# Block-sparse attention and top-2 experts on one core: a weight split, a ring of raw weights and the first gathers are put elsewhere in the order

## The chip, the cores and the metric

The kernel runs on one core of a Trainium2 chip. The metric is device time in microseconds (us) of one execution; the time before is the median of three runs. One execution was also recorded by the hardware profiler, and all rows below are from that one.

## The reference

Block-sparse attention first: 4 batches of 8 heads, 768 rows, 64 columns a head, in blocks of 32 rows. A block of queries sees its neighbours, the first and last block and three sampled ones; the first and last block see everything.

```python
scores = scale * np.matmul(q, k.transpose(0, 1, 3, 2))
scores = np.where(mask, scores, -1000000000.0)
attn = softmax(scores)
attn_out = np.matmul(attn, v)
```

Its 3072 rows of 512 go to eight experts, two for each row, chosen by noisy gate logits:

```python
for e in range(8):
    for k in range(2):
        mask = top2[:, k] == e
        h = np.maximum(x[mask] @ w1[e], 0.0)      # 512 -> 1024
        out[mask] += top2_w[mask, k, None] * (h @ w2[e])   # 1024 -> 512
```

## The kernel before, in words

**Order.** The kernel writes out its own order: every engine runs its instructions in program order, and transfers go out on two queues, SP's (`nc.sync`) and POOL's (`nc.gpsimd`), each in its own order too. A transfer that has to wait holds all that stands behind it on its queue.

**Attention.** `Attention.steps` (line 482) walks 64 items, 16 a batch (12 "q" items, two for each tile of 128 queries, and 4 "g" items), as a pipeline: step k makes the scores and the softmax of item k+2, transposes the probabilities of item k and multiplies item k-1 with the values (`av`, line 350, L361; global blocks in `global_av`, L384). The values of a tile lie in `va` and `vb`; `prefetch_v` (line 212) loads a tile in two halves, the second a step after the first, by eight to fourteen transfers on SP's queue (L229, L234). The last batch is steps 46 to 63, and its tiles of values 2 to 5 go out at steps 54, 56, 58 and 60, their second halves a step later. `prefetch_k` copies keys of a tile from `kk` into `kc` on POOL (L206). `kk` has two buffers, `kk0` for batches 0 and 2, `kk1` for batches 1 and 3 (line 92). At the end of a step, after all of this, `step` (spot 3) does what `plan` holds for that step. `at(n, f, ...)` puts something there. In the code `NS` is 64, `PER` 16, `EC` 53 and `M0` 57. The router's work on a finished batch is spread over the steps as a generator; batch 2's ends in step 57 with the table of rows for units 0 and 1 (`finish_table`, `r_gi`, L835).

**Experts.** `Experts.units` is a list of ten units, each some rows of one expert. Units 0 and 1 are experts 0 and 1 over the rows of batches 0 to 2, units 2 and 3 the same experts' rows of batch 3, and unit 4 (`FAST`, expert 2) is the fifth. A unit gathers its rows from `x_rows` into `xg` (`gather`, POOL's queue, L1004), transposes them by DMA into `xta` or `xtb` (`xpose`, SP's queue, L1014), and runs a first layer and a second (`mm2`, L1157 and L1166). From unit 4 on the first layer is `layer1_fast` (line 1085): 28 products of six matmuls each in the order of `PRODUCTS` (numbered 0 to 27 here), seven products a column group with sums of blocks, and eight hooks at which other work is issued (`HOOKS`: hook 0 after product 3, hook 1 after product 6, hook 2 after product 10). ACT copies some products out of PSUM (L1098, `ta` and `tc`), and a later product that adds into the same bank waits for that copy.

**Weights.** A piece of raw weights is 128 x 1024 fp32 (512 KB). `load_piece` (line 909) loads it on SP's queue into one of three buffers of the pool `wst`. `weight_sums` (L921, four DVE additions) makes block sums of a first-layer piece from expert 2 on, `high_piece` (L946, ACT) and `low_piece` (L950, DVE) split the piece into two fp16 parts, after which the next load may take the buffer. `do` (line 1468) issues a list of such operations by short names, and first the loads whose buffers came free since the last call. `FIRST_BACK` says what is issued behind the two chunks of unit 3's second layer; behind a chunk `back` puts the transposes of unit 5's rows first, and then that list.

Of the kernel before, what the change touches and what calls it, by code (L numbers as in the profile page):

```python
# [9 lines left out]
F32 = mybir.dt.float32  # L10
# [10 lines left out]
P = 128  # L21
# [27 lines left out]
class Attention:  # L49
# [3 lines left out]
    def __init__(self, tc, qt, qg, kt, vx, vw, vg, sampled, H, D):  # L53
        self.tc, self.nc = tc, tc.nc
        self.qt, self.qg, self.kt, self.vx, self.vw, self.vg, self.sampled = qt, qg, kt, vx, vw, vg, sampled
        self.B, self.T = qt.shape[:2]
        self.H, self.D = H, D
        self.NP = H // 2
        self.S = self.T * P
        self.NB = self.S // 32  # L60
        self.W = D + 4
        self.HD = H * D
        self.HW = H * self.W
        self.late_ = (self.B - 1) * self.T
        self.RB = 32 * self.HD * 4
        self.held_v = {}
        self.listed_rows, self.weights = {}, {}
        self.items = []
        for b in range(self.B):
            q = [("q", b, t, f) for t in range(self.T) for f in range(2)]  # L70
            g = [("g", b, i, par) for i in range(2) for par in range(2)]
            self.items += g[0:2] + q[0:1] + g[2:3] + q[1:2] + g[3:] + q[2:] if b == 0 else q[0:1] + g[0:3] + q[1:2] + g[3:] + q[2:]
        self.st = {}

    def open(self, ctx, early, ident):
        tc, nc = self.tc, self.nc
        pool = lambda c, name, bufs, **kw: c.enter_context(tc.tile_pool(name=name, bufs=bufs, **kw))
        self.const = pool(ctx, "aconst", 1, side="right")
        self.buf = pool(ctx, "abuf", 1, side="right")
        self.qp = pool(ctx, "aq", 3, side="right")  # L80
        self.pp = pool(ctx, "app", 2, side="right")
        self.gp = pool(early, "agp", 3)
        self.sm = pool(ctx, "asm", 4, side="right")
        self.xp = pool(ctx, "axp", 2, side="right")
        self.ps_s = pool(ctx, "ps_s", 3, space=PSUM)
        self.ps_o = pool(ctx, "ps_o", 2, space=PSUM)
        ep = pool(early, "aeb", 1)
        two = lambda n: ep if n == 2 else self.buf
        J = self.NJ
        self.va = [two(i).tile([P, J, self.HW], F32, name=f"va{i}") for i in range(3)]  # L90
        self.vb = [two(i).tile([P, J, self.HW], F32, name=f"vb{i}") for i in range(3)]
        self.kk = [two(2 - 2 * i).tile([P, self.NB, P], F32, name=f"kk{i}") for i in range(2)]
        self.kc = [self.buf.tile([P, J, self.NP, 8, 32], F32, name=f"kc{i}") for i in range(2)]
        self.qgt = [two(2 - 2 * i).tile([P, self.NP, 64], F32, name=f"qg{i}") for i in range(2)]
        self.ends = [two(2).tile([P, self.HD], F32, name=f"ends{i}") for i in range(2)]
        self.xs = [self.buf.tile([P, self.NP, 2, P], F16, name=f"x{n}") for n in range(2)]
        self.og = self.const.tile([P, 4, self.W], F32, name="og")
        self.known = self.const.tile([P, self.NB, 2], F32, name="known")
        self.pgt = [self.buf.tile([P, 8, P], F32, name=f"pgt{i}") for i in range(4)]
        self.ident = ident  # L100
        self.ident16 = self.const.tile([P, P], F16, name="a_ident16")
        nc.vector.tensor_copy(self.ident16, self.ident)
        nc.vector.memset(self.known, 1.0 / XS)
        self.zero = self.const.tile([P, 256], F32, name="zero")
        nc.vector.memset(self.zero, 0.0)
# [736 lines left out]


class Experts:
    def __init__(self, tc, router, w1, w2, out, x_dram):
        self.tc, self.nc, self.router = tc, tc.nc, router
        self.w = (w1, w2)
        self.out, self.x_dram = out, x_dram
        self.N, self.D = out.shape
        self.KB = self.D // P  # L850
        self.FB = 2 * self.KB
        self.st = {}

        self.units = [(0, 0, CA), (1, 1, CA), (E + 1, 1, CB), (E, 0, CB)] + [(e, e, C) for e in range(NH, E)]
        self.w1b, self.w2b, self.tb = {}, {}, {}
# [10 lines left out]
    def open_left(self, ctx):  # L866
        tc = self.tc
        pool = lambda name, bufs, **kw: ctx.enter_context(tc.tile_pool(name=name, bufs=bufs, **kw))
        self.wst = pool("wst", 3)
        self.w1s = [pool("w1s", 1)]  # L870
        self.xp = pool("mxp", 1)
        self.xta = pool("mxta", 1)
        self.xg = self.xp.tile([P, 7, 2 * self.D], F16, name="xg")
        self.first = self.xg[:, 5:7, 0:CA]
# [32 lines left out]
        return u >= FAST  # L907

    def load_piece(self, e, i):
        t = self.wst.tile([P, 2 * self.D], F32, name="wraw")  # L910
        self.nc.sync.dma_start(t, self.w[i // 4][e, i % 4])
        self.st["wraw", e, i] = t

# [397 lines left out]
def kernel(ctx, tc, qt, qg, kt, vx0, vx1, vx2, vx3, vw, vg, sampled_blocks, gates, noise, w1, w2, out):  # L1311
    nc = tc.nc
    N, DM = out.shape
    T = qt.shape[1]
    H = 2 * qt.shape[3]
    x_dram = nc.dram_tensor("x_rows", (N, 2 * DM), F16, kind="Internal").ap()
# [2 lines left out]
    nc.scalar.preload_act_table_set("natural_log_exp_and_others")  # L1319
    rp = ctx.enter_context(tc.tile_pool(name="route", bufs=1))  # L1320
    router = Router(tc, rp, N, DM, T, x_dram)
    ex = Experts(tc, router, w1, w2, out, x_dram)
    att = Attention(tc, qt, qg, kt, (vx0, vx1, vx2, vx3), vw, vg, sampled_blocks, H, DM // H)
    late, early, left, right, first = (ExitStack() for _ in range(5))
    att.open(late, early, router.ident)
    router.hot = late.enter_context(tc.tile_pool(name="hot", bufs=1, side="right"))
    jobs = []

# [5 lines left out]
    def background(count=1):  # L1334
        for _ in range(count):
            if jobs and next(jobs[0], jobs) is jobs:
                jobs.pop(0)

    NS = len(att.items)
    PER = NS // att.B  # L1340
    EC = PER * 3 + 5
# [7 lines left out]
    at = lambda n, f, *a: plan.setdefault(n, []).append((f, a))  # L1349
# [4 lines left out]
    for i in range(8):  # L1354
        at(PER + 7 + 3 * i, fill_out, i)
    for i in range(3):
        at(EC + 1 + i, ex.load_piece, 0, i)
    at(NS - 4, ex.split_piece, 0, 0)
    at(NS - 3, ex.load_piece, 0, 3)
    M0 = NS - 7  # L1360
    at(M0, ex.meta, 0)
    at(M0 + 1, ex.meta, 1)
    for c in range(ex.count(0)):
        at(M0 + 2 + c // 2, gather_early, c)
        at(M0 + 3 + c // 2, ex.xpose, 0, c)

    for i in range(2):
        at(i - 2, router.consts, i)
# [5 lines left out]
    def step(n, spot):  # L1374
# [6 lines left out]
        for f, a in plan.get(n, []):  # L1381
# [22 lines left out]
    GATHERS = (((2, 0), (2, 1)), ((3, 0), (3, 1)), ((4, 4), (4, 5)), ((4, 6), (4, 0)), ((4, 1), (4, 2)))  # L1404
    FIRST_ROWS = ((), (), (), (("rs", 0, 0),), (("rs", 0, 1),), (("rd", 0, 0),), (("rd", 0, 1),),
                  (("rh", 0), ("rs", 1, 0), ("rs", 1, 1), ("rd", 1, 0), ("rd", 1, 1), ("rl", 0), ("rh", 1)))
    FIRST_BACK = ((("rl", 1), ("s2", 2), ("h2", 2), ("l2", 2)), (("s2", 3), ("h2", 3)))
    SPLITS = ((1, 2), (3,), (4,), (5,), (6,), (7,), (), ())
    queue = [(e, i) for e in range(E) for i in range(8)]

# [7 lines left out]
    def split(e, i):  # L1418
        ex.split_piece(e, i)
        next_load(e, i)  # L1420

    def low(e, i):
        ex.low_piece(e, i)
        freed.append((e, i))

    def front(u, f):
        nn = ex.count(u + 1) if u + 1 < nu else 0
        if u == 0:
            for i in SPLITS[f]:
                split(0, i)  # L1430
            background(UB if f else 0)
            if 1 <= f <= nn:
                ex.gather(1, f - 1)
            if 2 <= f <= nn + 1:
                ex.xpose(1, f - 2)
        if u == 1:
            if f < 3:
                background(UB if f < 2 else 200)
            else:
                ex.gather_prev(1, [f - 3])  # L1440
            if f == 4:
                nc.gpsimd.memset(ex.xg[:, C // P], 0.0)
                for v in (2, 3, 4):
                    ex.meta(v)
        if u == 2:
            if f == 1:
                ex.gather(4, 3)
            if FAST + 1 + f < nu:
                ex.meta(FAST + 1 + f)
        if u == 3:  # L1450
            if f in (2, 3):
                ex.gather_prev(3, [3 - f])
            for c in ((0, 1), (2, 3), (), (), (4,), (5,), (6,), ())[f]:
                ex.gather(5, c)
            do(u, FIRST_ROWS[f])
        if u == FAST:
            if f == 0:
                low(2, 3)
            if f > 3:
                ex.gather_prev(u, ex.chunks(u)[2 * f - 8:2 * f - 6])  # L1460
        if u == nu - 1 and f == 3:
            nc.gpsimd.drain()
        if u >= FAST:
            do(u, FRONT[f])
            if nn:
                do(u, FRONT_ROWS[f])
# [23 lines left out]
    def back(u, k, n):  # L1490
# [17 lines left out]
        if u == 3:  # L1508
            for c in range(4 * k, 4 + 3 * k):
                ex.xpose(5, c)  # L1510
            do(u, FIRST_BACK[k])
        if u >= FAST and nn:
# [4 lines left out]
    for u in range(nu):  # L1517
        left_ = ex.rows(u)[1]
        n = ex.count(u)
# [64 lines left out]
```

## Time and profile before

| | us |
|---|---|
| runs | 847.37, 847.04, 841.62 |
| median | 847.04 |
| the profiled execution | 847.43 |
| its span, first to last instruction | 845.6 |

Mean granted TensorE clock 0.978. Busy shares: PE 93%, DVE 69%, ACT 47%, POOL 46%. In the rows "[3.06 <-issue]" at the end of a line is the idle time of that engine ahead of it and what ended it; "issue" is time in which the engine waited for nothing that the profile shows. SPq is SP's DMA queue: the duration on its rows is that of the issue, not of the transfer.

### The profile page before, as it was taken

To read this page: it belongs to the slowest core of one execution; us is meant where nothing else is said; L and a number is where in the kernel's file an instruction comes from. 1 tells how busy PE (TensorE), PEld (TensorE's weight loads), DVE (VectorE), ACT (ScalarE), POOL (GpSimd) and SP (SyncE) were. 2 spreads that over 40 slices of the span, in tenths; PEclk is the share of its full clock that TensorE was granted. 3 is DMA by queue.
4 is the path that set the end of the run, shared out by engine and by line. 5 is a ranking of instruction groups with operands and counts; after the bars stand their busy time and mean duration, and the time that the engine had idled before them with its cause. 6 is when DMAs were issued, how large, how long until landed. Compare 5 with 4: busy or idle time off the path is not lost.

```text
span 845.6 us, 24928 instructions
## 1 busy us (share of the span) xinstructions
PE 782.9 (93%) x9799; PEld 481.0 (57%) x9799; DVE 581.6 (69%) x1161; ACT 400.3 (47%) x736; POOL 391.9 (46%) x679
## 2 busy tenths in 40 slices
PE   7899879978977689999997999999999999999995
PEld 4576556656655566465684554554554554555552
DVE  6766687778779557752438796796796796796621
ACT  5868848846853545221214543543543443443500
POOL 5684876757645440231634345245255255233211
PEclk8999999999988999999999999999999999999998
DMA  8766787897727979541979557557557557523211
GB/s 237 209 200 204 227 242 238 250 281 199 211 76 215 234 183 246 188 133 41 241 155 185 180 146 208 167 159 195 165 164 198 167 161 195 167 89 115 90 38 44
DMA packets 118305, 148.87 MB, mean 176 GB/s; under 512 B 69515, under 2 KB 76300, under 8 KB 118178
## 3 DMA queue, kind: packets, MB, share of 16 engines
q1 hardware_dynamic: 104034, 102.93, 46.4%
q0 software_dynamic: 14144, 44.25, 16.0%
q8 instruction: 79, 1.29, 0.7%
q14 instruction: 48, 0.39, 0.2%
HBM read 107.28 MB, written 26.15 MB: 158 GB/s over the span
## 4 chain that ended last, share of the span: by engine, by line
PE 78%; DVE 9%; ACT 5%; issue 4%; SPq 1%; DMA 1%; POOL 1%; POOLq 0%; DVEq 0%; ACTq 0%
PE pc L1157 29%; PE pa L1110 12%; PE ps L266 6%; PE pd L1110 6%; PE po L361 5%; PE ps L333 4%; PE pa L1071 4%; PE pc L1110 3%; PE pc L1166 2%; PE pd L1071 2%; PE po L384 2%; DVE m L303 2%; ACT p L306 2%; PE ps L319 1%; DMA vb<-in_vx_dram 1%
## 5 line engine op out<-in xcount | busy, mean ns | idle before, releaser
L1157 PE MATMUL pc<-w,hh 128*128 128x512 f16 x758 | 225.4, 379 | 0.0
L1190 POOL DMA_INDIRECT out_dram<-y,r_xT x46 | 64.4, 1400 | 216.5 <-DVE y L1189 178.3
L1110 PEld LDWEIGHTS <-w 128*128 128x128 f16 x1008 | 99.1, 98 | 80.6 <-issue 5.8
L1157 PE MATMUL pc<-w,hl 128*128 128x512 f16 x379 | 143.6, 379 | 0.0
L1157 PEld LDWEIGHTS <-hh 128*128 128x128 f16 x758 | 73.5, 98 | 85.6
L306 ACT ACTIVATE p<-ps,m 128x256 f32<-128x256 f32 x192 | 75.3, 476 | 60.2 <-DVE m L303 49.1
L206 POOL COPY kc<-kk 128x128 f32 x264 | 68.6, 299 | 47.0 <-PE ps L266 39.1
L303 DVE TENSOR_REDUCE m<-ps 128x4 f32<-128x1024 f32 x48 | 58.6, 1220 | 28.8 <-PE ps L266 28.7
L1004 POOL DMA_INDIRECT xg<-x_rows,r_xT x46 | 60.5, 1315 | 14.0 <-issue 13.7
L266 PE MATMUL ps<-kc,q 64*32 64x256 f32 x1536 | 58.2, 398 | 9.2 <-issue 5.2
L361 PE MATMUL po<-va,ptr 128*32 128x68 f32 x1536 | 56.0, 232 | 11.0 <-issue 5.8
L950 DVE SCALAR_TENSOR_TENSOR w<-wraw,w 128x1024 f16<-128x1024 f32 (+1 forms) x58 | 64.4, 1110 | 1.4 <-ACT w L946 1.4
L361 PE MATMUL po<-vb,ptr 128*32 128x68 f32 x1536 | 55.9, 228 | 8.0 <-issue 6.0
L1022 POOL DMA_INDIRECT pv<-out_dram,r_xT x44 | 49.8, 1133 | 28.8 <-issue 21.3
L1157 PEld LDWEIGHTS <-hl 128*128 128x128 f16 x379 | 37.0, 98 | 44.8
L1110 PE MATMUL pa<-tb,w 128*128 128x408 f16 x288 | 56.6, 340 | 3.8 <-ACT ta L1098 3.8
L946 ACT ACTIVATE w<-wraw 128x1024 f16<-128x1024 f32 (+1 forms) x58 | 55.7, 960 | 5.1 <-DMA wraw<-in_moe_w_dram 5.1
L1189 DVE SCALAR_TENSOR_TENSOR y<-pc,r_xT,pv 128x512 f32<-128x512 f32 x37 | 27.7, 749 | 43.6 <-PE pc L1157 43.6
L1110 PE MATMUL pd<-tb,w 128*128 128x408 f16 x288 | 56.5, 336 | 0.0
L333 PE MATMUL ps<-r_ident,p 128*128 128x128 f32 x384 | 53.9, 284 | 0.0
L361 PEld LDWEIGHTS po<-va,ptr 128*32 128x32 f32 x1536 | 39.3, 113 | 21.9 <-issue 10.1
L1079 ACT ACTIVATE hh<-pa 128x408 f16<-128x408 f32 (+2 forms) x55 | 23.8, 443 | 59.1 <-PE pa L1071 52.6
(246 smaller groups left out, 1547.6 us busy)
## 6 DMA issues: line engine op xcount, KB each, us to landing
wraw<-in_moe_w_dram SPq DMA_DIRECT2D x64, 512.0 KB, 3.9
va<-in_vw_dram SPq DMA_DIRECT2D x40, 384.0 KB, 4.7
vb<-in_vx_dram SPq DMA_DIRECT2D x176, 64.0 KB, 3.6
q<-in_qt_dram SPq DMA_DIRECT2D x24, 256.0 KB, 3.9
out_dram<-zero SPq DMA_DIRECT2D x8, 768.0 KB, 5.2
va<-in_vx_dram SPq DMA_DIRECT2D x88, 64.0 KB, 4.2
kk<-in_kt_dram SPq DMA_DIRECT2D x18, 256.0 KB, 4.9
x_rows<-x POOLq DMA_DIRECT2D x16, 256.0 KB, 4.2
```

The costliest lines, as they stand in the source:

```text
L206: nc.gpsimd.tensor_copy(kc[:, j, :, 3 + n], flat[:, bass.ds(self.listed(blk, n), P)].rearrange("p (n c) -> p n c", c=32))
L266: mm = lambda o, l, r: nc.tensor.matmul(o, l, r, start=True, stop=True, skip_group_check=True)
L303: nc.vector.tensor_reduce(m, s.rearrange("p a (e c) -> p a e c", e=2), axis=AX.X, op=ALU.max, negate=True)
L306: i = nc.scalar.activation(p[:, 2 * e + par], s[:, par, 256 * e:256 * e + 256], AF.Exp, bias=m[:, par, e:e + 1])
L333: self.apart(it, par, nc.tensor.transpose(t[:, e, c], p[:, 2 * e + par, P * c:P * c + P], self.ident))
L361: nc.tensor.matmul(o[32 * j:32 * j + 32, h], d[:, h % 2, h // 2, x, 32 * j:32 * j + 32], self.values(v[:, self.slot(t, j)], 4 * f + h), st ...
L946: self.nc.scalar.activation(hi, t, AF.Copy, scale=WS)
L950: self.nc.vector.scalar_tensor_tensor(lo, t, WS, hi, op0=ALU.mult, op1=ALU.subtract)
L1004: nc.gpsimd.indirect_dma_start(out=self.xg[0:m, c + self.place(u)], out_offset=None, in_=self.x_dram[0:nr], in_offset=bass.IndirectOffsetO ...
L1110: nc.tensor.matmul(o, w[:, wt, slot, s * P:s * P + P], mv(s, a), start=i == 0 and p in tail, stop=i == 5, skip_group_check=True)
L1157: nc.tensor.matmul(py, self.hidden[f][h][:, o], w(f)[:, x], start=i == 0, stop=i == last)
L1190: d = nc.gpsimd.indirect_dma_start(out=self.out, out_offset=bass.IndirectOffsetOnAxis(ap=r["ix"][0:m, c:c + 1], axis=0), in_=y[0:m], in_of ...
```

## The change

Five edits. The three buffers for raw weights are one tile now, allocated at the start, and the old `kk0` is a view of the same memory. The loads of expert 0's pieces 0 to 2 go from the ends of steps 54 to 56 to those of 48 to 50, that of piece 3 from step 61 to 63. The gathers of unit 0's five chunks go from steps 59, 59, 60, 60, 61 to 57, 57, 58, 58, 59. Its five transposes go from steps 60, 60, 61, 61, 62 to 60, 61, 61, 61, 62. In unit 3 and 4, the sums and the high part of expert 2's piece 3 leave unit 3's last list; the sums are issued at hook 0 of unit 4, the high and the low part at hook 1 (the low part stood at hook 0).

```diff
-    def open(self, ctx, early, ident):
+    def open(self, ctx, early, ident, raw):
...
-        self.kk = [two(2 - 2 * i).tile([P, self.NB, P], F32, name=f"kk{i}") for i in range(2)]
+        self.kk = [raw.rearrange("p a (n c) -> p (a n) c", c=P), self.buf.tile([P, self.NB, P], F32, name="kk1")]
...
+        self.raw, self.loads = raw, 0
...
-        self.wst = pool("wst", 3)
...
-        t = self.wst.tile([P, 2 * self.D], F32, name="wraw")
+        t = self.raw[:, self.loads % 3]
+        self.loads += 1
...
+    raw = ctx.enter_context(tc.tile_pool(name="raw", bufs=1)).tile([P, 3, 2 * DM], F32, name="wraw")
...
-        at(EC + 1 + i, ex.load_piece, 0, i)
+        at(PER * 3 + i, ex.load_piece, 0, i)
     at(NS - 4, ex.split_piece, 0, 0)
-    at(NS - 3, ex.load_piece, 0, 3)
+    at(NS - 1, ex.load_piece, 0, 3)
...
-        at(M0 + 2 + c // 2, gather_early, c)
-        at(M0 + 3 + c // 2, ex.xpose, 0, c)
+        at(M0 + c // 2, gather_early, c)
+        at(NS - 4 + (c + 2) // 3, ex.xpose, 0, c)
...
-    FIRST_BACK = ((("rl", 1), ("s2", 2), ("h2", 2), ("l2", 2)), (("s2", 3), ("h2", 3)))
+    FIRST_BACK = ((("rl", 1), ("s2", 2), ("h2", 2), ("l2", 2)), ())
...
         if u == FAST:
-            if f == 0:
-                low(2, 3)
+            if f < 2:
+                do(u, ((("s2", 3),), (("h2", 3), ("l2", 3)))[f])
```

## Rows read from the trace of the kernel before

**Rows 1.** The page: the chain's shares by engine, and the costliest groups of L1110.
```profile
PE 78%; DVE 9%; ACT 5%; issue 4%; SPq 1%; DMA 1%; POOL 1%; POOLq 0%; DVEq 0%; ACTq 0%
...
L1110 PE MATMUL pa<-tb,w 128*128 128x408 f16 x288 | 56.6, 340 | 3.8 <-ACT ta L1098 3.8
```
**Rows 2.** Windows: busy time (instructions) by engine, then PEclk, DMA share, GB/s.
```profile
235.00:250.00 15.00, 10.28 (x220) 7.47 (x217) 9.02 (x41) 8.05 (x19) 6.38 (x19) 0.77 0.10 37
...
295.00:300.00 5.00, 4.08 (x75) 3.73 (x78) 1.62 (x5) 1.79 (x3) 0.67 (x1) 0.66 1.10 305
...
460.00:464.00 4.00, 3.62 (x13) 1.66 (x13) 3.03 (x4) 2.66 (x5) 0.39 (x1) 0.57 1.18 196
```
**Rows 3.** Timeline of PE, last steps of attention: start, duration, instruction, [idle before].
```profile
277.98 0.25 PE L361 MATMUL po<-vb,ptr 128*32 128x68 f32 x1 [0.58 <-DMA vb<-in_vx_dram]
...
288.33 0.22 PE L361 MATMUL po<-vb,ptr 128*32 128x68 f32 x1 [1.41 <-DMA vb<-in_vx_dram]
...
295.92 0.32 PE L361 MATMUL po<-vb,ptr 128*32 128x68 f32 x7 [3.06 <-issue]
...
303.44 0.25 PE L361 MATMUL po<-va,ptr 128*32 128x68 f32 x1 [1.38 <-issue]
```
**Rows 4.** DMA queues between 288.4 and 293.1: packets, MB, share (only two queues ran).
```profile
q1 hardware_dynamic: 795, 0.51, 69.0%
q0 software_dynamic: 165, 0.51, 40.0%
```
**Rows 5.** DMA queue of instructions between 293.1 and 294.3.
```profile
q8 instruction: 1, 0.02, 5.6%
```
**Rows 6.** DMA queue of instructions between 300.8 and 302.1 (none from 296.0 to 300.8).
```profile
q8 instruction: 1, 0.02, 5.5%
```
**Rows 7.** Timeline of SP's queue: issues.
```profile
268.62 0.41 SPq L911 DMA_DIRECT2D wraw<-in_moe_w_dram  x1
...
288.28 4.86 SPq L1014 DMA_TRANSPOSE xta<-xg  x2
293.19 0.57 SPq L229 DMA_DIRECT2D va<-in_vw_dram  x1
...
296.11 6.40 SPq L1014 DMA_TRANSPOSE xta<-xg  x3
...
461.07 6.44 SPq L911 DMA_DIRECT2D wraw<-in_moe_w_dram  x3
```
**Rows 8.** Timelines of DVE and POOL: the table's last step, the first gather.
```profile
272.46 0.62 DVE L835 TENSOR_SCALAR r_gi<-r_ix 128x16 int32<-128x16 int32 x1
...
279.16 1.12 POOL L1004 DMA_INDIRECT xg<-x_rows,r_gi  x1 [0.17 <-issue]
```
**Rows 9.** Timeline of PE, unit 4: products 2, 3, 12 and 14.
```profile
455.35 1.20 PE L1110 MATMUL pc<-xta,w 128*128 128x408 f16 x6
460.38 2.20 PE L1110 MATMUL pa<-tb,w 128*128 128x408 f16 x6 [3.84 <-ACT ta L1098]
...
471.21 1.20 PE L1110 MATMUL pa<-xta,w 128*128 128x408 f16 x6
...
473.28 1.20 PE L1110 MATMUL pc<-xta,w 128*128 128x408 f16 x6
```
**Rows 10.** Timeline of ACT, the same stretch: high parts and copies.
```profile
454.71 0.83 ACT L946 ACTIVATE w<-wraw 128x768 f16<-128x768 f32 x1
458.88 1.06 ACT L946 ACTIVATE w<-ws 128x1024 f16<-128x1024 f32 x1 [3.34 <-DVE ws L921]
459.84 0.89 ACT L1098 ACTIVATE ta<-pa 128x408 f32<-128x408 f32 x2
...
466.64 1.05 ACT L946 ACTIVATE w<-wraw 128x1024 f16<-128x1024 f32 x1
```
**Rows 11.** Timeline of DVE, the same stretch: the first and last of four sums.
```profile
457.30 0.41 DVE L921 TENSOR_TENSOR ws<-wraw 128x256 f32<-128x256 f32 x1
...
458.43 0.42 DVE L921 TENSOR_TENSOR ws<-wraw,ws 128x256 f32<-128x256 f32 x1
```
**Rows 12.** The tile wraw: loads, issue to landing.
```profile
DMA to landing us min/median/max: 3.2/3.9/5.5
```

More of the change, by code (lines that the diff above doesn't have):

```diff
@@ L844, with __init__ @@
 class Experts:
-    def __init__(self, tc, router, w1, w2, out, x_dram):
+    def __init__(self, tc, router, w1, w2, out, x_dram, raw):
         self.tc, self.nc, self.router = tc, tc.nc, router
@@ L1321 @@
     router = Router(tc, rp, N, DM, T, x_dram)
-    ex = Experts(tc, router, w1, w2, out, x_dram)
+    raw = ctx.enter_context(tc.tile_pool(name="raw", bufs=1)).tile([P, 3, 2 * DM], F32, name="wraw")
+    ex = Experts(tc, router, w1, w2, out, x_dram, raw)
     att = Attention(tc, qt, qg, kt, (vx0, vx1, vx2, vx3), vw, vg, sampled_blocks, H, DM // H)
     late, early, left, right, first = (ExitStack() for _ in range(5))
-    att.open(late, early, router.ident)
+    att.open(late, early, router.ident, raw)
     router.hot = late.enter_context(tc.tile_pool(name="hot", bufs=1, side="right"))
```

## The prediction

> **What bounds the kernel now.** I read the page's chain first: 78% of it is PE, and PE is busy 93% of the span [rows 1]. So an edit is worth only what PE stands still for, or what its clock loses. The second view is a set of 5 us windows, searched for stretches where PE is not full beside the edited code. There are two: the last steps of attention (273 to 304) and the head of unit 4 (455 to 464). From 315 to 455 and behind 464 PE is full, so time won at either place is kept. The third view is PE's timeline in those two places, for what ended each idle time; the fourth are the queues that the edits touch.
>
> At the end of attention PE waits 0.58 and 1.41 us for values [rows 3], then stops twice in the middle of a run of equal matmuls whose data is there, 3.06 and 1.38 us, for "issue" [rows 3]. The queue of instruction blocks explains these: from 288.4 to 293.1 only data queues ran [rows 4], a block came in at 293.1 to 294.3 [rows 5], and PE went on at 295.92; the next came behind 300.8 [rows 6], and PE went on at 303.44. Both times DMA transposes were being issued: two from 288.28 for 4.86 us, three from 296.11 for 6.40 [rows 7]. I read it as PE's next block of instructions held up by transposes. The clock then falls: 0.66 from 295 to 300 [rows 2], so 0.34 x 5 = 1.7 us at the half level behind the long stop.
>
> In unit 4 PE stands 3.84 us ahead of product 3, for ACT's copies `ta` [rows 9]. ACT is late because the high part of piece 3 sits in front of them: its second half waited 3.34 us for the DVE sums and ran at 458.88 [rows 10], the sums ran at 457.30 to 458.85 [rows 11]. The clock is 0.57 from 460 to 464 [rows 2]: 0.43 x 4 = 1.7, less 0.2 for the 0.38 us still idle, so 1.5 us.
>
> **The change part by part.** *The split in unit 4.* Without the sums and high part in front, ACT copies `ta` from 454.8 (its earlier high part ends there, where the removed 454.71 row starts [rows 10]). Product 3 then follows product 2 at once: a product takes (473.28 - 471.21) / 2 = 1.035 us [rows 9], so it starts at 455.35 + 1.03 = 456.38, 4.0 us earlier, and no clock falls. What is late next? The same work comes back at hooks 0 and 1: sums of 1.55 us on DVE [rows 11], high parts of 0.83 + 1.06 us on ACT [rows 10], the low part moved by one hook. DVE has room: PE needs nothing of it at once. ACT has a knot. Behind the new high part, hook 1 issues the high part of piece 5, whose raw load stands on SP's queue behind seven transposes and goes out at 461.07 [rows 7] whatever PE does. With a landing of 3.9 us [rows 12] that is 465.0. Before, ACT came there at 466.64 and did not wait [rows 10]; now it comes there at about 464 and does. Its 1.05 us and a copy of some 0.45 (half of the 0.89 for two [rows 10]) end at 466.5, and that copy frees the bank of product 11. Without a stall product 11 would start at 456.38 + 8 x 1.035 = 464.66, so PE stands 1.85 us. Product 14 starts at 466.5 + 3 x 1.035 = 469.6 in place of 473.28 [rows 9]: 3.7 us won. Bounds: with no wait 473.28 - (456.38 + 11 x 1.035) = 5.5; with the longest landing, 5.5 us [rows 12], 2.1, and 0.6 if the clock falls as it did at 460. I take 3.7, from the median landing.
>
> *Loads of pieces 0 to 2 to steps 48 to 50.* `kk0` is last read by batch 2's scores and copies, steps before 48, so the loads need not wait. They add three issues of some 0.4 us [rows 7] to SP's queue near 225 to 232, ahead of query tiles needed 20 us later, and 1.5 MB that fall largely into 235 to 250, where the DMA share is 0.10 [rows 2]: nothing to pay, unless an instruction block is late there too (rival below). What they leave is the crowded stretch: the one issued at 268.62 [rows 7] stood right ahead of the values for which PE waits 0.58 us at 277.98 [rows 3]. I take 0.6 us won. The 1.41 us at 288.33 may also shrink, but beside it DVE and ACT do a split of their own that PE waits for next, so I count nothing; bounds 0 and 2.0.
>
> *Gathers two steps sooner.* The table is there at 273.1 [rows 8], in the very step that now holds the first gathers; POOL waits up to 0.8 us for it, and five gathers of 1.1 us plus 0.3 us gaps delay POOL's other work by 3 to 4 us, which is needed five or more microseconds later. On the DMA side the gathers move from 279 to 288 into 273 to 282, while 0.5 MB of weights leave: by 288 the sum is less than before. I take 0 (bounds: -0.6, as the first transposes need not wait, and +0.6, the wait at 277.98 kept).
>
> *Transposes behind v; piece 3 last.* Each transpose takes about 2.4 us of SP (4.86 / 2 [rows 7]). One instead of two now goes ahead of the last half tile of values (293.19 [rows 7]); four stand behind it, and the load of piece 3, needed only in unit 0, behind them all. The first block of instructions now meets one transpose, not two, so I expect it some 2.4 us sooner: the 3.06 us go nearly, and with them the 1.7 us of clock. The second block then meets three to four transposes in a row. PE would want it at 292.9 - 0.6 + (302.06 - 295.92) - 1.7 = 296.7, in the midst of them. I price this as one stop like the long one, 3.1 us, in the place of the 1.38, and half of its lost clock, 0.85, since what follows waits for DVE and ACT anyway. Sum for the end of attention: 0.6 + 3.06 + 1.7 + 1.38 - 3.1 - 0.85 = 2.8 us. Bounds: 6.8 with both blocks in time; about 0 with both as late as now.
>
> Two rules of the Trainium skill speak against this part. "Runtime: NRT & Kernel Launch", section Instruction fetch mechanics, says that the sequencer fetches its next block over its own DMA queue while it runs the present one, and that the cost of crossing a block is mostly hidden; "DMA: Bandwidth & Descriptors", section Queues, rings and completion order, says that an engine takes turns between queues packet by packet. By these a block would not wait for whole transposes, their order would not matter, and the sum would be that of the second rival below; the stops at 292.9 and 302.1, which end behind the blocks of 293 and 301, do not agree.
>
> **Sum.** 3.7 + 2.8 = 6.5 us. Against the profiled execution's own 847.4 (span 845.6) that is 840.9. The median of the runs, 847.04, is 0.4 lower, and one of the three runs was 841.62, so a spread of some 5 us comes without any edit; a stop with its clock costs just that much, 3.06 + 1.7.
>
> **The rivals.** *All stops gone*: blocks in time and ACT not held, 6.8 + 5.5 = 12.3, so 835.1. For it: removed loads and a lone first transpose thin the traffic. Against: the same five transposes still run within 15 us, and the 461.07 issue does not move. *The stops only move*: the end of attention wins just the 0.6, so 0.6 + 3.7 = 4.3 and 843.1. For it: transposes are as many as before. *The change doesn't do what it says in unit 4*: ACT's knot moves from product 3 to product 11 in full, with the clock; 2.8 remain, 844.6. For it: the late 461.07; against: it needs a landing of 7.5 us, longer than any of 64 loads [rows 12]. *Slower*: PE's instruction blocks become late at new places, in 228 to 240, where 1.5 MB more are loaded, and in 273 to 282, where the gathers now meet the loads of values. A stop like the long one costs 3.06 + 1.7 = 4.8. It decides from the second new stop on: two, with nothing won at the end of attention, give 847.4 + 9.6 - 3.7 = 853.3, three 858.1. For it: "issue" is 4% of the chain already [rows 1]; against: a DMA share of 0.10 there [rows 2].
>
> **How the numbers follow.** Forecast 0.42, all gone 0.24, only moved 0.14, not in unit 4 0.10, slower 0.10. A measurement of this kernel can tell about 1%, 8.5 us, from no change: below 838.6 lie nearly all of "all gone" and a piece of the forecast (its own range is 838 to 844), together 0.30; slower by over 1% only the worse half of the last, 0.05; 0.65 between. The range takes in the first rival down to 834.5 and reaches to 849, above the third; what lies outside is 0.15.
>
> **What would show it.** Right: product 3 follows product 2 with no wait for `ta`; a short wait at product 11 for ACT; no long "issue" stop between the last half of values and the second run of transposes, one stop some 5 us later; no weights on SP's queue from 250 to 290. Wrong: "issue" stops between 228 and 282 that were not there; ACT idle for `wraw` over 2 us in unit 4; a wait of unit 0's first tile for `xta`.

## The result, and the profile after

| kernel | median, us (lowest to highest) | runs |
|---|---|---|
| before | 846.94 (841.62 to 850.85) | 10 |
| changed | 840.49 (838.12 to 844.58) | 10 |

The ratio on record is 0.9917, with a 95% interval of 0.9893 to 0.9941; the quotient of the two medians is 0.9924. That is 7.0 us less by the ratio and 6.45 between the medians, where 6.5 were forecast. The profiled execution of the changed kernel took 844.58 us (span 842.7), the longest of its ten, and that of before 847.43. So the two traces differ by only 2.9 us, and some 4 us of what the median shows can't be looked for in them. This matters below: one half of the forecast came out as worked out, the other half did not, and the total fits all the same.

**Unit 4.** PE's timeline of the changed kernel: products 2, 3, 11 and 14, which answer to [rows 9].

```profile
456.17 1.20 PE L1111 MATMUL pc<-xta,w 128*128 128x408 f16 x6
457.21 1.20 PE L1111 MATMUL pa<-tb,w 128*128 128x408 f16 x6
...
467.41 1.20 PE L1111 MATMUL pa<-tb,w 128*128 128x408 f16 x6 [1.76 <-ACT tc L1099]
...
470.52 1.20 PE L1111 MATMUL pc<-xta,w 128*128 128x408 f16 x6
```

The 3.84 us ahead of product 3 are gone: it starts 1.04 us behind product 2. The new wait is where it was forecast, at product 11, 1.76 us for ACT. From product 2 to product 14 it is 14.35 us now and was 17.93: 3.58 won. What held ACT stands in its own timeline and in SP's.

```profile
465.91 1.06 ACT L947 ACTIVATE w<-wraw 128x1024 f16<-128x1024 f32 x1 [1.02 <-DMA wraw<-in_moe_w_dram]
```

```profile
443.85 17.45 SPq L1015 DMA_TRANSPOSE xtb<-xg  x7
461.39 31.26 SPq L912 DMA_DIRECT2D wraw<-in_moe_w_dram  x7
```

The raw load goes out at 461.39, behind seven transposes, and ACT waits 1.02 us for it. The clock keeps its full level: the window 460 to 464, 0.57 before [rows 2], shows 1.00.

```profile
305.00:310.00 5.00, 5.00 (x31) 3.13 (x30) 0.65 (x3) 0.20 (x1) 3.39 (x5) 0.66 0.51 182
460.00:464.00 4.00, 4.00 (x25) 2.28 (x24) 2.41 (x7) 2.74 (x6) 0.11 (x1) 1.00 1.08 232
```

**The end of attention.** Here the first of the two windows above is the worse one: 0.66 from 305 to 310, in unit 0. PE's timeline of the changed kernel shows why; it answers to [rows 3].

```profile
277.56 0.25 PE L361 MATMUL po<-vb,ptr 128*32 128x68 f32 x1 [0.93 <-DMA vb<-in_vx_dram]
...
283.37 0.25 PE L361 MATMUL po<-va,ptr 128*32 128x68 f32 x2 [1.64 <-issue]
...
288.66 0.31 PE L361 MATMUL po<-va,ptr 128*32 128x68 f32 x2 [1.51 <-DMA va<-in_vx_dram]
...
304.80 4.97 PE L1072 MATMUL ps<-xta,w1s 128*128 128x320 f16 x23 [3.47 <-DMA xta<-xg]
```

Both long stops for issue, 3.06 and 1.38 us, are gone, the second one too. The stop that ends at 283.37 isn't new: the kernel before stops at the same place for 0.45 us (below). In place of the long stops unit 0's first tile waits 3.47 us for its transposed rows. The chain of waits from 290 to 310 leads from the values on SP's queue through the transposes to that tile (start, duration, what).

```profile
293.92 0.37 SPq L234
...
294.39 1.44 SPq L1015
...
295.92 1.30 SPq L1015
...
297.31 2.15 SPq L1015
...
299.55 5.20 DMA xta<-xg
304.75 0.05 issue
304.80 4.99 PE ps L1072 x23
```

The last transpose is issued at 299.55, and its rows land 5.20 us later, at 304.75. Now the kernel before: PE's timeline with the short stop and the same tile, and then, from the view of the tile `xta`, its last transpose.

```profile
282.61 0.25 PE L361 MATMUL po<-va,ptr 128*32 128x68 f32 x1 [0.45 <-issue]
...
304.73 3.42 PE L1071 MATMUL ps<-xta,w1s 128*128 128x320 f16 x24
```

```profile
L1014 SPq DMA_TRANSPOSE xta<-xg x1: 2322/2322/2322, 300.2 to 300.2; - x1
...
DMA to landing us min/median/max: 4.3/4.3/4.3
```

Its rows landed at 300.2 + 4.3 = 304.5 there and at 304.75 here, and it started at 304.73 there and at 304.80 here. The stops were taken away and the first tile didn't move: PE now reaches it at 301 and stands until the rows are there, the clock falls behind that wait, and unit 0 runs 5 us at 0.66, where the kernel before had 1.00 in the same window:

```profile
305.00:310.00 5.00, 4.58 (x40) 2.97 (x37) 3.05 (x9) 2.09 (x5) 1.89 (x4) 1.00 0.00 0
```

From the end of PE's wait at L809 (258.97 before, 258.31 after) to product 2 of unit 4 (455.35 and 456.17) it is 196.38 us before and 197.86 after: 1.5 us longer, not 2.8 shorter.

### The profile page after: what moved, and what is told of

Read it like the earlier page. It is cut to its first block, busy times and chain, and to the rows that moved or that the text cites. A ratio compares the mean times of both kernels' runs of the same rounds, so it can differ in the third digit from the quotient of the medians.

```text
span 842.7 us, 24931 instructions
## 1 busy us (share of the span) xinstructions
PE 780.6 (93%) x9799; PEld 480.4 (57%) x9799; DVE 581.7 (69%) x1161; ACT 400.5 (48%) x736; POOL 390.5 (46%) x679
## 4 chain that ended last, share of the span: by engine, by line
PE 75%; DVE 10%; ACT 6%; DMA 4%; issue 3%; SPq 1%; POOL 0%; DVEq 0%; POOLq 0%; ACTq 0%
PE pc L1158 29%; PE pa L1111 11%; PE pd L1111 6%; PE ps L266 5%; PE po L361 5%; PE pa L1072 4%; PE ps L333 3%; PE pc L1111 3%; PE pc L1167 2%; DMA vb<-in_vx_dram 2%; PE pd L1072 2%; DVE m L303 2%; PE po L384 2%; ACT p L306 2%; PE ps L319 1%
## 5 line engine op out<-in xcount | busy, mean ns | idle before, releaser
L361 PE MATMUL po<-va,ptr 128*32 128x68 f32 x1536 | 56.1, 230 | 12.0 <-issue 5.3
L361 PE MATMUL po<-vb,ptr 128*32 128x68 f32 x1536 | 56.1, 227 | 6.3 <-issue 4.4
L1190 DVE SCALAR_TENSOR_TENSOR y<-pc,r_xT,pv 128x512 f32<-128x512 f32 x37 | 27.7, 749 | 43.6 <-PE pc L1158 43.6
L361 PEld LDWEIGHTS po<-va,ptr 128*32 128x32 f32 x1536 | 39.7, 112 | 24.2 <-issue 10.5
L1072 PEld LDWEIGHTS <-w1s 128*128 128x128 f16 x432 | 42.4, 99 | 17.1 <-DMA xta<-xg 3.7
```

What stands on the lines that cost most here:

```text
L361: nc.tensor.matmul(o[32 * j:32 * j + 32, h], d[:, h % 2, h // 2, x, 32 * j:32 * j + 32], self.values(v[:, self.slot(t, j)], 4 * f + h), st ...
L1072: nc.tensor.matmul(ph[:, 0:m], w[:, wt, slot, kb % 2 * P:kb % 2 * P + P], r["xt"][:, kb, a, o:o + m], start=i == 0, stop=i == last)
```

## The experiments

Each kernel ran beside the kernel before on its own chip, and only ratios are compared; chips differ (before took 862.49 us on that of e1 to e4, 861.84 on that of e5 to e8 and 848.40 on that of f1 to f4). The ratios are those on record; the quotients of the medians differ from them by up to 0.0028 (0.9976 for e2), but lie inside each interval. Every kernel left one profile, that of one execution.

| kernel | median, us | ratio, 95% interval |
|---|---|---|
| changed, again (e5) | 854.70 | 0.9906 [0.9871, 0.9942] |
| split alone (e1) | 859.19 | 0.9963 [0.9934, 0.9992] |
| end of attention alone (e2) | 860.41 | 1.0004 [0.9968, 1.0040] |
| end of attention alone, again (f1) | 847.86 | 0.9988 [0.9960, 1.0016] |
| changed, transposes at old steps (e3) | 854.01 | 0.9928 [0.9894, 0.9961] |
| the same, again (e6) | 854.17 | 0.9900 [0.9859, 0.9941] |
| changed, load between transposes (e4) | 857.32 | 0.9928 [0.9894, 0.9962] |
| changed, loads at old steps (e7) | 857.96 | 0.9956 [0.9924, 0.9988] |
| split and early loads (f2) | 841.70 | 0.9909 [0.9874, 0.9943] |
| changed, transposes sooner (f3) | 846.26 | 0.9970 [0.9945, 0.9996] |

**The two halves by themselves.** The kernel before with the split's edit alone:

```diff
-    FIRST_BACK = ((("rl", 1), ("s2", 2), ("h2", 2), ("l2", 2)), (("s2", 3), ("h2", 3)))
+    FIRST_BACK = ((("rl", 1), ("s2", 2), ("h2", 2), ("l2", 2)), ())
...
-            if f == 0:
-                low(2, 3)
+            if f < 2:
+                do(u, ((("s2", 3),), (("h2", 3), ("l2", 3)))[f])
```

> The kernel before with only the move of piece 3's sums, high and low part to hooks 0 and 1 of unit 4. Theory A (both parts of the change pay, the split 3.6 us and the rest about 2.9 us of the 6.45 us between the medians): 3.6 us below before, a ratio near 0.996; product 3 of unit 4 starts 1.03 us behind product 2 with no wait, and PE waits 1.5 to 2 us ahead of product 11. Theory B (all of the median's gain is the split): 6.4 us below, 0.992. Theory C (the split's place hides nothing): 1.000.

0.9963 of 862.49 is 3.2 us: the size of the 3.58 in the trace. Its profile shows something else as well. Its end of attention is that of the kernel before, and still the stop of 3.06 us isn't there. PE waits for ACT instead, and of the stops for issue only the later one is of a microsecond (PE's timeline):

```profile
297.53 2.08 PE L384 MATMUL po<-va,pgt 96*64 96x68 f32 x32 [2.38 <-ACT r_xT L436]
...
306.91 0.25 PE L361 MATMUL po<-va,ptr 128*32 128x68 f32 x1 [1.13 <-issue]
```

So a stop that is missing from one trace need not have been taken away by an edit. The changed kernel with those two edits undone, and all else kept, twice:

> The change without the move of piece 3: raw ring in the old key tile, loads, gathers and transposes as after. Theory A: 2.9 us below before, ratio near 0.9965, with the 3.84 us wait of PE ahead of product 3 still there. Theory B: 1.000, as the one profiled execution of the change suggests, where the end of attention was 0.8 us later than before because the first tile waited 3.47 us for its transposed rows. A third: slower by up to 2 us, if that wait is there in every execution.

> The part of the change at the end of attention, without the split's move, a second time. The first time it gave a ratio of 1.000, while the whole change less the split alone leaves some 4 us for it. Theory A (the end of attention gives nothing: the wait for unit 0's rows takes what the issue stops cost): ratio 0.999 to 1.001 again. Theory B (the prediction's 2.8 us): ratio 0.997 or below. Theory C (the two parts help each other, the whole is more than their sum): 1.000 here, and the whole stays at 0.991.

1.0004 and 0.9988: nothing that can be measured, where 2.8 us (a ratio of 0.9967) had been forecast. The second interval by itself still reaches that far, the two together hardly. The traces agree: from the last matmuls at L809 (261.00 in the kernel before) to the first tile it is 43.3 to 45.4 us in the six profiles with the new end of attention (changed, e2, e4, e5, f1, f4), and 43.7 and 43.6 in the two with the old one (before, e1). PE's timeline of f1 has both marks, the wait for unit 0's rows of the changed kernel, and the wait for `ta` of before:

```profile
305.56 4.63 PE L1072 MATMUL ps<-xta,w1s 128*128 128x320 f16 x17 [4.11 <-DMA xta<-xg]
...
462.46 1.20 PE L1111 MATMUL pa<-tb,w 128*128 128x408 f16 x6 [3.84 <-ACT ta L1099]
```

So the wait for `ta` belongs to the old split also behind the new end of attention, and the wait for `xta` to the new end of attention. In e2's profile, where unit 3 ran late, the first of them is 2.22 us and the second 3.57. The split's worth changes with it: from product 2 to product 14 it is 16.48 us in e2 and 13.66 in e1 on the one chip, 2.8 less, and 18.10 in f1 and 13.73 in f2 on the other, 4.4 less.

**The changed kernel again.** No edit.

> The changed kernel once more, beside its own variants. Theory A (the split gives 3.2 to 3.7 us, the end of attention gives nothing on balance because the wait for unit 0's transposed rows takes the place of the issue stops): 3 to 4 us under the kernel before, ratio 0.996, and the profile shows PE waiting over 1 us for xta again. Theory B (the end of attention gives 2.8 us as the prediction had it, and the one profiled execution happened to be a poor one): 6 to 7 us under before, ratio 0.992, and PE waits less than 1 us for xta.

Neither theory came out whole. The profile has the wait for `xta` again, so the trace of the first one was no accident:

```profile
306.37 2.06 PE L1072 MATMUL ps<-xta,w1s 128*128 128x320 f16 x8 [3.49 <-DMA xta<-xg]
```

Its size varies: with the same end of attention it is 1.20 us in e4 and 1.78 in f4.

The ratio, 0.9906, is nevertheless that of the rival with the good end of attention. The two halves measured alone add up to 1 - (0.0037 + 0.0004) = 0.9959, with the mean of 1.0004 and 0.9988 for the second; the whole was 0.9917 and 0.9906. The gap of some 4 us is about as large as the intervals of the parts together. Whether the halves help each other or the parts were measured a little low isn't settled; the split had less to win on the chip of e1 and e2 than on that of f1 and f2, which may fill some of the gap.

**The transposes.** Moved back to the steps of before, on two chips:

```diff
-        at(NS - 4 + (c + 2) // 3, ex.xpose, 0, c)
+        at(M0 + 3 + c // 2, ex.xpose, 0, c)
```

> The change with unit 0's transposes put back to steps 60, 60, 61, 61, 62 (two ahead of the last half tile of values). If the order of transposes is what wins at the end of attention: 2 to 5 us slower than the change, ratio to before 0.994 to 0.998, and stops for issue near 292 again. If only the sooner gathers and loads win: the same as the change, 0.9917. If one more transpose in front helps the first tile (its wait for xta of 3.47 us goes): up to 2 us faster than the change, 0.9895.

> The changed kernel with unit 0's transposes back at their old steps, beside the changed kernel itself. Theory A (the later transposes cost what they free): 2 to 4 us below the changed kernel of the same chip, as the wait for xta goes and the sooner gathers keep the issue stops away. Theory B (the transposes were the cause of the issue stops, wherever they run beside the values): equal to the changed kernel or up to 3 us above it, with stops for issue of over 1 us back between 285 and 305 us.

0.9928 and 0.9900 stand on either side of the changed kernel's 0.9906 on comparable chips: the order of the transposes and the values makes no difference that shows. The stop of 2.42 us in the second profile is what its theory B expected, but the first, of the same kernel, has no stop for issue of half a microsecond there. In the first of these two profiles the first tile waits 0.29 us for its rows, in the second 2.61. PE's timelines, first and second:

```profile
303.04 3.30 PE L1072 MATMUL ps<-xta,w1s 128*128 128x320 f16 x23 [0.29 <-DMA xta<-xg]
```

```profile
288.44 0.32 PE L361 MATMUL po<-va,ptr 128*32 128x68 f32 x2 [2.42 <-issue]
...
308.27 2.05 PE L1072 MATMUL ps<-xta,w1s 128*128 128x320 f16 x7 [2.61 <-DMA xta<-xg]
```

From the last matmuls at L809 to the first tile it is 42.0 us in the first and 46.7 in the second, for one and the same kernel: so much a single profile of this stretch can be off.

Then ahead of both kernels' places:

```diff
-        at(NS - 4 + (c + 2) // 3, ex.xpose, 0, c)
+        at(NS - 5 + c // 2, ex.xpose, 0, c)
```

> The changed kernel with unit 0's transposes at steps 59, 59, 60, 60, 61, ahead of both kernels' places. Theory A (the first tile waits 1.6 to 3.9 us for transposed rows because they are issued behind the values): the wait for xta falls below 1 us and the ratio is 0.986 to 0.989. Theory B (transposes that run beside the values hold up values and instruction blocks): the wait for xta goes but stops of over 1 us for issue or for values come between 283 and 300 us, and the ratio is 0.991 or above.

Theory B: 0.9970, worse than the changed kernel. The first tile doesn't wait any more, but it is later than in any of the others on chips of this speed, at 307.32, since PE had already stood for values and for instructions (PE's timeline):

```profile
283.79 0.25 PE L361 MATMUL po<-va,ptr 128*32 128x68 f32 x2 [2.65 <-issue]
...
300.51 0.44 PE L361 MATMUL po<-va,ptr 128*32 128x68 f32 x4 [3.93 <-DMA va<-in_vx_dram]
...
307.32 1.97 PE L1072 MATMUL ps<-xta,w1s 128*128 128x320 f16 x8
```

And without them, the five replaced by plain copies:

```diff
+        if u == 0:
+            self.nc.sync.dma_start(r["xt"][:, :, :, c * P:(c + 1) * P].rearrange("p k a r -> p (k a) r"),
+                                   self.x_dram[c * P:(c + 1) * P].rearrange("p (n r) -> p n r", r=P))
+            return
         self.nc.sync.dma_start_transpose(out=r["xt"][:, :, :, c * P:(c + 1) * P].rearrange("p k a r -> p (k a) r"),
```

> Unit 0's five transposes are replaced by plain copies of 256-byte runs of x_dram's rows: the transposition and the gathered order are left out for unit 0. Theory A (the transposes hold up PE's instruction blocks and come late themselves): no wait for xta at unit 0's first tile, no stop for issue over 1 us between 280 and 305 us, and no stretch of over 1 us in which the DMA engines stand around an instruction packet there. Theory B (the traffic as such does it): stops for issue of over 1 us stay, or the DMA still stands about 1.3 us after an instruction packet.

This kernel leaves out the transposition and the gathered order, so it only serves for its trace; its one run, 852.22 us, lies within the changed kernel's twelve on that chip (848.35 to 860.13). The signs of theory A are there. But one of them decides nothing: there is no stop for issue of a microsecond between 280 and 305, and e5, on the same chip and with the transposes, has none of even half a microsecond there. The first tile waits 0.43 us, against 3.49 in e5:

```profile
302.58 3.30 PE L1076 MATMUL ps<-xta,w1s 128*128 128x320 f16 x23 [0.43 <-DMA xta<-x_rows]
```

The DMA view tells most: its two rows are the DMA engines' busy tenths and what they moved, in 40 slices of 0.2 us. First the changed kernel, 296 to 304; then the same kernel on the chip of the copies (e5), 296 to 304; then the copies, 297 to 305.

```profile
DMA  9959999999700003999999988999900000099999
GB/s 236 134 97 198 282 299 206 229 193 54 3 3 8 10 10 72 288 279 278 269 234 212 173 162 159 289 174 74 12 0 0 8 10 9 10 244 289 444 533 430
```

```profile
DMA  9989748998799999990000099999999799999980
GB/s 379 297 338 359 297 126 224 233 174 95 128 279 277 235 211 209 143 23 0 8 9 10 10 259 287 264 270 238 211 201 189 147 218 211 210 279 165 196 9 0
```

```profile
DMA  9999999999999999986159699999599861001000
GB/s 269 274 338 214 392 297 316 328 255 274 293 269 268 269 253 238 201 150 112 24 182 223 161 326 366 369 410 451 225 307 389 328 225 41 20 0 20 0 20 0
```

With transposes the engines moved almost nothing for 1.0 us from 298.0 and for 1.4 us from 301.6, and in e5 for 1.0 us from 299.6; each time an instruction block had been fetched just before (the instruction queue has one packet between 297 and 298 and one between 301 and 301.6, and in e5 one between 298.5 and 299). The holes lie in the way of the transposes, the second of the changed kernel's between the last issue and the landing at 304.75. With copies, and two blocks in 8 us as there, no such hole comes until the work runs out near 303.6. So the holes are shown to go with the transposes. That PE's stops for issue go with them is not shown.

**The early loads.** Pieces 0 to 2 back at their old steps, in the changed kernel; and, the other way round, early loads and split with gathers and transposes as before:

```diff
-        at(PER * 3 + i, ex.load_piece, 0, i)
+        at(EC + 1 + i, ex.load_piece, 0, i)
```

> The changed kernel with the loads of pieces 0 to 2 back at steps 54 to 56. Theory A, the prediction's 0.6 us: 0 to 1 us above the changed kernel, one more wait of about half a microsecond for values near 278 us. Theory B (1.5 MB less traffic in the last steps of attention is what the change lives on): 3 us or more above it, with stops for issue or values of over 1 us between 270 and 300 us.

```diff
-        at(M0 + c // 2, gather_early, c)
-        at(NS - 4 + (c + 2) // 3, ex.xpose, 0, c)
+        at(M0 + 2 + c // 2, gather_early, c)
+        at(M0 + 3 + c // 2, ex.xpose, 0, c)
```

> Split moved and pieces 0 to 2 loaded at steps 48 to 50; gathers and transposes of unit 0 at their old steps. Theory A (the early loads carry what the end of attention gives): ratio 0.990 to 0.993, as the whole change. Theory B (gathers or transposes carry it): 0.996, as the split alone.

0.9956 without the early loads against 0.9906 with them, on one chip, and 0.9909 with the early loads but neither of the other two moves. So gathers and transposes carry nothing that shows, and the early loads look like 4 us (0.0050 of 855; 3.3 between the medians), with intervals of 0.003 on each side. By the time that is theory B of the first and theory A of the second. The first has the stop that its theory B expected (PE's timeline):

```profile
288.33 0.32 PE L361 MATMUL po<-va,ptr 128*32 128x68 f32 x1 [2.53 <-issue]
```

But e6, which has the early loads, has the like of it, 2.42 us at 288.44, and a ratio of 0.9900. Both kernels here also keep the load of piece 3 at step 63 and the raw weights in the memory of `kk0`, which no run moves alone. PE's timeline of the second: both of the old stops for issue [rows 3] are still there, but shorter, and the first tile starts without a wait.

```profile
261.46 1.28 PE L809 MATMUL po<-hot 128*128 128x256 f16 x4 [3.36 <-DVE hot L800]
...
296.03 0.33 PE L361 MATMUL po<-vb,ptr 128*32 128x68 f32 x8 [1.04 <-issue]
299.93 0.31 PE L361 MATMUL po<-va,ptr 128*32 128x68 f32 x4 [1.87 <-DMA va<-in_vx_dram]
...
304.06 0.25 PE L361 MATMUL po<-va,ptr 128*32 128x68 f32 x2 [0.71 <-issue]
305.35 1.93 PE L1072 MATMUL ps<-xta,w1s 128*128 128x320 f16 x13
```

3.06 + 1.38 - 1.04 - 0.71 = 2.7 us, with a new wait of 1.87 us for values between them. From the wait at L809, 3.36 us in these three profiles, to the first tile it is 43.9 us here, 45.8 before (from 258.97) and 46.5 in the changed kernel (from 258.31): 1.9 us won in this profile, less than the 4.7 us between the profiles of e3 and e6. Against this stand the two runs of the end of attention alone, which have the early loads too and gained nothing. It stays open.

**The knot at product 11.** In the changed kernel the load of piece 5 was sent between the transposes of unit 5, two of seven behind it:

```diff
             for c in range(4 * k, 4 + 3 * k):
+                if c == 5:
+                    do(u, ())
                 ex.xpose(5, c)
```

> The change with the load of expert 2's piece 5 put on SP's queue between unit 5's transposes 4 and 5 instead of behind 6. Theory (ACT's wait for that load is what holds product 11): the 1.02 us wait of ACT for wraw goes, PE's wait ahead of product 11 falls from 1.76 to about 0.7 us, and the time is 1.0 us below the change, ratio near 0.9905. Rival (ACT's own work holds product 11): the wait stays at 1.5 to 1.8 and the time at 0.9917. A loss of 1 us or more would say that the load in front makes unit 5's rows late.

Inconclusive. On this chip unit 3 ran late for all kernels, so the raw load was in time anyway, in the split-alone kernel too. PE's timeline of either kernel has the same short wait at product 11, here this one's and then the split-alone's:

```profile
481.24 1.20 PE L1111 MATMUL pa<-tb,w 128*128 128x408 f16 x6 [0.57 <-ACT tc L1099]
```

```profile
479.79 1.20 PE L1110 MATMUL pa<-tb,w 128*128 128x408 f16 x6 [0.57 <-ACT w L946]
```

The other runs tell more, because the load's lateness varied by itself. ACT's wait for `wraw` and PE's wait at product 11 were 1.02 and 1.76 us in the changed kernel, 0.34 and 1.09 in f2, 1.84 and 2.59 in f3, none and 0.65 in f4: the one sets the other, 0.74 to 0.75 behind it. Without the load's wait 0.57 to 0.65 us stay in e1, e4, e7 and f4, together with 0.34 to 0.38 at product 12 for DVE; in e3, e5 and e6 PE has no wait to speak of at product 11 and only the 0.35 at product 12.

**Where PE's stops for issue sit.** The changed kernel with 72 matmuls ahead of the first step instead of 40:

```diff
-        for _ in range(40):
+        for _ in range(72):
```

> The changed kernel with 72 in place of 40 matmuls ahead of the first step, which moves all of PE's later stream by 64 instructions. Theory A (PE's stops for issue sit at the ends of blocks of 256 instructions, a property of the stream): the stops fall 64 instructions of the program earlier, at the same counts from the start of the stream (192 above a multiple of 256). Theory B (they sit at certain steps of the program): they stay with the same matmuls, at counts 64 higher.

Theory A (its one run took 841.85 us). Windows from one wait of PE to the next (time, then busy time and count of PE and of its weight loads): before from 292.7, the changed kernel from 276.5, this one from 280.4. All end at a stop for issue, and two begin with one; that of the changed kernel begins with the wait at 277.56, which the profile puts down to values.

```profile
292.70:301.90 9.20, 5.64 (x134) 4.95 (x125) 2.73 (x9) 2.23 (x4) 0.68 (x3) 0.81 1.39 225
```

```profile
276.50:281.60 5.10, 4.17 (x129) 3.13 (x127) 2.89 (x6) 3.69 (x8) 4.11 (x7) 1.00 0.99 305
```

```profile
280.40:286.40 6.00, 4.51 (x131) 3.45 (x128) 4.02 (x7) 3.83 (x8) 2.44 (x4) 1.00 1.03 229
```

259, 256 and 259 instructions, with a few cut by the edges: one block of 256 each, though the times differ. Counted from the start of each of the fourteen traces (matmuls, weight loads and PE's own waiting instructions), every stop for issue of 0.7 us or more up to 307 us falls 193 or 194 above a multiple of 256, in this kernel too. Some of the shorter ones, and those in unit 3 shown at the end, fall elsewhere. And with 64 instructions more in front, the stop of the changed kernel at 283.37, ahead of values (L361), came ahead of another operation (PE's timeline of this kernel):

```profile
282.06 0.57 PE L384 MATMUL po<-va,pgt 96*64 96x68 f32 x11 [1.49 <-issue]
...
289.50 0.57 PE L361 MATMUL po<-va,ptr 128*32 128x68 f32 x5 [2.94 <-issue]
```

## Why the prediction was right, and where it wasn't

*The split, 3.7 us: right, 3.58.* Product 3 follows at once, and the clock stays. The wait of 1.85 us at product 11 was 1.76, for the reason given: the raw load behind seven transposes. That it came within 0.1 us is in part luck: with the load's lateness the wait ran from none to 2.59 us in the other profiles. The upper bound, 5.5 with no wait, was reached in none; the nearest is e5 with 13.10 us from product 2 to product 14, 4.8 less than the 17.93 before. The rival that nothing would be won in unit 4 falls.

*Loads, 0.6 us: the place was wrong.* The wait at 277.98 that was to go is still there, 0.93 us at 277.56. The load of 268.62 hardly stood in its way: the values that ended that wait went out on SP's queue only from 273.49, 4.9 us later, and such a load lands in 3.9 us at the median [rows 12]. The runs point to more than 0.6 us for the loads, through shorter issue stops at 296 and 304, but the runs of the second half alone disagree, so their size is open.

*Gathers, 0: nothing in the runs speaks against it.* With gathers and transposes at their old steps the ratio is the same, 0.9909.

*Transposes, first block: it came out, but not shown to be by the order.* No stop ends near 296 in the changed kernel's two traces; the 3.06 us and the half clock behind them are gone. But e1, with all of the old order, and e3 and e6, with the transposes at their old steps, have none there either. And without the stop the first tile starts no sooner.

*Transposes, second block: this step failed.* The prediction said that the second block would stop PE for 3.1 us with 0.85 us of clock. There is no such stop in the changed kernel's trace. What came was a wait of the first tile for `xta`, 3.47 us (1.20 to 4.11 in the other runs with this end of attention), with 0.66 of the clock for 5 us, 1.7 us, behind it. It had been named as a sign of being wrong but had no price. The price could have been read: [rows 7] has the last transposes on SP's queue from 296.11 to 302.51, their rows landed at 304.5, and the first tile started at 304.73. The change leaves the last transpose at the same step, and now its issue ends at 300.83 and its rows land at 304.75, 3.9 us behind. The stops hid that the rows were no sooner. With the stop at 283.37, 1.64 us in place of 0.45, the end of attention lost 1.5 us in the profiled execution, and it gave nothing in the two runs of that half alone.

*The sum.* 6.5 us forecast and 6.45 between the medians; but of the parts only the 3.6 of unit 4 are shown. The rest, about 3 us, comes with the early loads by two comparisons and doesn't come in the two runs of the end of attention alone; its cause is open, and that the total fits is luck as far as the runs show. The rival of new late instruction blocks between 228 and 282 isn't seen: no stop for issue of 0.4 us lies there in the changed kernel's trace, and the one that ends at 283.37 was there before and grew by 1.2 us, where the rival needed two of 4.8. The rule of the Trainium skill, "Runtime: NRT & Kernel Launch", section Instruction fetch mechanics, that crossing a block is mostly hidden, agrees with the trace of the kernel before for most blocks: up to 304 us PE runs some 48 of them and stops for issue for 0.7 us or more at eight. These eight, 0.7 to 3.5 us each, are the rest that it leaves.

No version beats the changed kernel clearly: f2 and e6 equal it. If one is to be kept, f2 does with fewer moves.

## What to carry to other kernels

Before counting a stall as won, look for what the instruction behind it needs and when that comes: here PE was past its stops just when the transposed rows landed (304.5 us), so taking them away moved the wait by some instructions and not the work. Follow a new critical step's inputs back through their queue and add the landing time, as was done for the raw load in unit 4 (and came out to 0.1 us in that trace) and not for unit 0's rows. And a total that fits is no proof of its terms: try the halves alone. Nor is a stop that is gone from one trace a proof of what took it away: look whether it is there in a second profile without the edit.

## What was not expected of the hardware

PE's stops for issue of 0.7 us or more up to 307 us all come 256 of its instructions apart or a multiple of that, so an edit that only adds instructions early moves them to other operations; at which of these places PE stops, and for how long, differs from one execution to the next. A block that came among several running DMA transposes was followed by 1.0 to 1.4 us in which the DMA engines moved almost nothing, at the end of attention and, 1.2 us from 450.2, in unit 5's transposes; with copies in the transposes' place it wasn't, nor at 498.1 us, with a single transpose under way.

Chips differ more than the change is worth, and in good part at one place: on the two slower chips PE also stands in unit 3, in every kernel profiled there, and the two others show nothing of it. PE's timeline of the changed kernel on one of them:

```profile
445.63 1.02 PE L1072 MATMUL pa<-xtb,w 128*128 128x224 f16 x9 [2.53 <-DVE hl L1084]
...
450.67 2.40 PE L1072 MATMUL pa<-xtb,w 128*128 128x224 f16 x12 [2.99 <-issue]
```

What causes it wasn't tried.
